# One POOL queue for the first batches' loads, in order of need, and their transposes and scalings reordered, in a fused attention and feed-forward kernel on one Trainium2 core

## The chip, the cores and the metric

The kernel runs on one core of one Trainium2 chip. A core has TensorE (PE in the profile; PEld is its weight load), VectorE (DVE), ScalarE (ACT), GpSimd (POOL) and SyncE (SP), and 16 DMA engines that serve the queues of all of them. The metric is the time on the device in microseconds. For a program on one core it is the time of that core.

## The reference

The inputs are q, k and v of 8 batches with 8 heads, 576 positions and 64 elements a head, gates s of 8 x 8 x 576, and the two weights of a feed-forward layer (512 x 2048 and 2048 x 512). All are float32.

```python
scores = q @ k.T / 8
cum = cumsum(max(s, 0))                      # along the positions
bias = -(cum[i] - cum[j])
scores = where(j > i, -1e9, scores + minimum(bias, 0))
attn = exp(scores - rowmax); attn = attn / (sum(attn) + 1e-9)
x = attn @ v                                 # heads side by side: 4608 tokens x 512
out = gelu_exact(x @ w_in) @ w_out           # 4608 x 512
```

Since the scores are causal, the bias factors into a weight of the key, exp(cum[j]), which cancels the query's share when the row is normalised. The kernel therefore multiplies v and a row of ones by that weight (`wb`), and never forms the bias.

## The kernel before

**Tiling.** The eight heads of a batch form four pairs (`NP`), and one item of work covers a pair: transposes, scores, mask, products with v. The 576 positions are five tiles (`ST`), four of 128 and one of 64. The feed-forward layer runs over 9 chunks (`NCH`) of 512 tokens. Chunk c needs the attention of batch c, and a part of the batch before. The program's order is written out by hand, and every engine and every queue works through its own share of it in that order.

**Loads.** q and k come through POOL's queue, which casts them to bf16 (`load_early`, L105). One call loads one pair, or two pairs with `both`. v comes through SP's queue in float32, one transfer a tile (`load_v`, L183), into two buffers (tag `rawv`). The weights also come through POOL's queue, cast to bf16 (`load_w`, L228). Each kind of queue has eight completion semaphores, so a transfer waits for the one eight before it in its queue to land. Three small copies into `pace` on POOL, and one into `raw_v` (L539), only wait for something and so hold back what follows them in POOL's queue or, through `raw_v`, in SP's.

**Batches 0 and 1.** `tr_item` transposes q or k of one pair on PE: 18 transposes into PSUM (L340), and a copy by DVE into `qkT` (L345). From batch 2 on, DVE rearranges q and k into rows (`interleave`, L156), SP writes those to DRAM (`write_rows`, L165) and reads them back through transposing DMAs (`transpose_rows`, L172).

**Attention of a pair.** `sc_item` makes the scores in two units, each with an Exp on ACT (L363), and masks their diagonal blocks with DVE or POOL (`mask_item`, L372 and L377). `scale_v` multiplies v by its weight on DVE (L211). `av_item` makes numerator and denominator for positions 0 to 511 (L385), and `norm` divides through Ln and Exp on ACT (L402, L403) and a product on DVE into `xT` (L418). `av_rest` and `norm_rest` do the same for positions 512 to 575 of all pairs.

**Feed-forward.** `l1_item` makes two column tiles of the first product (L463) and their Gelu on ACT (L469, L472). `l2_item` makes the second product for 128 tokens (L482), wholly or for some of its 16 steps; after the last step DVE copies it out of PSUM (L489) and SP writes it (L491). In chunks 1 to 6 these products use PSUM tag `mlp`, which has one buffer. Scores and first products share tag `sc` (2 buffers), and transposes, attention products and some others share tag `av` (3 buffers).

**Order of a chunk.** The first layer stands first. Beside it DVE scales v of the next batch, takes maxima of v, q and k (`absmax_v`, L201; `absmax`, L194), and interleaves the batch after next. Then comes the second layer, with the attention of batch c + 1 between its products.

Of the kernel before, what the change touches and what calls it, by code (L numbers as in the profile page):

```python
# [19 lines left out]
def kernel(  # L20
# [10 lines left out]
    nc = tc.nc  # L31
    fp32 = mybir.dt.float32
# [9 lines left out]
    ST = 5  # L42
# [53 lines left out]
    def load_early(b, n, p, both=False):  # L96
        src = q if n == "q" else k
        if p == 0:
            early[b, n] = work.tile([128, 2, 2, G * D], bf16, tag=f"raw{n}", bufs=3, name=f"early_{n}")
        e0 = (p // 2) * 64  # L100
        out = early[b, n][e0 : e0 + 64, p % 2]
        if both:
            out = early[b, n][e0 : e0 + 64].rearrange("g j e f -> g (j e) f")
        ap = [[G * D, 64], [S * D, 4 if both else 2], [1, G * D]]
        nc.gpsimd.dma_start(  # L105
            out=out,
            in_=bass.AP(tensor=src.tensor, offset=src.offset + (b * H + 2 * p) * S * D, ap=ap),
        )
# [5 lines left out]
    for p in range(1, NP):  # L114
        for n in "qk":
            load_early(0, n, p)
    uptri = const.tile([128, 128], fp32, name="uptri")
    make_upper_triangular(nc, uptri, 1.0, diag=True)
    ident_bf = const.tile([128, 128], bf16, name="ident_bf")
    nc.vector.tensor_copy(ident_bf, ident)  # L120
    one = const.tile([64, S], bf16, name="one")
    nc.vector.memset(one, 1.0)
# [12 lines left out]
    for t in vv:  # L135
        nc.vector.memset(t[64:128, ST - 1, :, :], 0.0)
    for t in qkT:
        nc.vector.memset(t[:, 1, :, S:640], 0.0)
# [6 lines left out]
    def load_qk(b):  # L145
        for p in (0, 2):
            for n in "qk":
                load_early(b, n, p, both=True)
# [25 lines left out]
    def v_tile(b):  # L174
        raws[b, "v"] = work.tile([128, ST, H, D], fp32, tag="rawv", bufs=2, name="raw_v")

    def load_v(b, engs):
        if (b, "v") not in raws:
            v_tile(b)
        t = raws[b, "v"]  # L180
        for st in range(ST):
            n_st = 128 if st < ST - 1 else SL
            engs[st % len(engs)].dma_start(  # L183
                out=t[:n_st, st, :, :],
                in_=bass.AP(
                    tensor=v.tensor,
                    offset=v.offset + b * H * S * D + st * 128 * D,
                    ap=[[D, n_st], [S * D, H], [1, D]],
                ),
            )  # L190
# [306 lines left out]
    load_v(0, [nc.sync])  # L497
    exp_set()
    pace = const.tile([128, 1], fp32, name="pace")

    def tr_pair(b, p):
        tr_item(b, p, 0)
        tr_item(b, p, 1)
# [4 lines left out]
    weights_scan()  # L508
    tr_pair(0, 0)
    weights_dve()  # L510
    nc.vector.tensor_copy(tri_bf, uptri)
    sc_item(0, 0, masks=False)
    mask_item(0, 0, 0, nc.vector)
    mask_item(0, 0, 1, nc.gpsimd)
    nc.gpsimd.tensor_copy(pace, raws[0, "v"][:, ST - 3, 0, 0:1])
    for i in range(4):
        load_w(0, i)
    tr_pair(0, 1)
    weights_pe()
    sc_item(0, 1, masks=False)  # L520
    mask_item(0, 1, 1, nc.gpsimd)
    tr_pair(0, 2)
    mask_item(0, 1, 0, nc.vector)
    sc_item(0, 2, masks=False)
    mask_item(0, 2, 1, nc.gpsimd)
    tr_pair(0, 3)
    sc_item(0, 3, masks=False)
    scale_pair(0, 0)
    mask_item(0, 2, 0, nc.vector)
    scale_pair(0, 1)  # L530
    mask_item(0, 3, 0, nc.vector)
    mask_item(0, 3, 1, nc.vector)
    scale_pair(0, 2)
    scale_pair(0, 3)
    for i in range(4):
        load_w(1, i)
    load_qk(1)
    v_tile(1)
    nc.gpsimd.tensor_copy(  # L539
        raws[1, "v"][:, :, 0, 0], w_in_r[:, KO - 1, dff - 1 : dff].to_broadcast([128, ST])  # L540
    )
    load_v(1, [nc.sync])
    for p in range(NP):
        av_item(0, p, wide=p in (1, 2), rest=False)
    nc.gpsimd.memset(amv, 0.0)
    nc.gpsimd.memset(ones, 1.0)
    nc.gpsimd.tensor_copy(pace[:64], raws[1, "v"][:64, ST - 1, 0, 0:1])
    load_qk(2)
    load_qk(3)

    for c in range(NCH):
# [3 lines left out]
        if c == 0:  # L555
            for p in range(NP):
                av_rest(0, p)
            norm_rest(0)
# [3 lines left out]
        if 0 < c and nb < B:  # L562
            if nb + 1 < B:
                load_v(nb + 1, [nc.sync])
            scale_v(nb, STS, nc.vector)
            absmax_v(nb)
# [5 lines left out]
        if 0 < c and nb + 1 < B:  # L572
            for i, n in enumerate("qk"):
                interleave(nb + 1, n)
                write_rows(nb + 1, i, nc.sync)
            if nb + 2 < B:
                nc.gpsimd.tensor_copy(
                    pace, qkT[nb % 2][:, 1, NP - 1, 0:1] if c == 1 else gT_of[c][:, 0, 0:1]
                )
                load_qk(nb + 2)  # L580
        for f2 in range(3, FT // 2):
            l1_item(c, f2)
        if c == 0:
            exp_set()
            l2_item(c, 0, av=True)
            tr_pair(1, 0)
            tr_pair(1, 1)
            l2_item(c, 1, 0, 4)
            tr_pair(1, 2)
            l2_item(c, 1, 4, 8)  # L590
            tr_pair(1, 3)
            sc_item(1, 0)
            l2_item(c, 1, 8)
            load_v(2, [nc.sync])
            sc_item(1, 1)
            l2_item(c, 2, 0, 6, av=True)
            sc_item(1, 2)
            scale_pair(1, 0)
            l2_item(c, 2, 6, 12, av=True)
            sc_item(1, 3)  # L600
            l2_item(c, 2, 12, av=True)
# [24 lines left out]
        elif nb < B:  # L626
            exp_set()
            l2_item(c, 0, 0, 4)
            sc_item(nb, 0)
            l2_item(c, 0, 4)  # L630
            for p in range(1, NP):
# [5 lines left out]
                if p == NP - 1:  # L637
                    if nb + 1 < B:
                        transpose_rows(nb + 1, p)
                    av_item(nb, p)  # L640
# [160 lines left out]
```

## Time and profile before

| | |
|---|---|
| median of 17 runs | 341.06 us (340.38 to 343.04) |
| time of the profiled execution | 341.79 us |
| its span, first to last instruction | 339.9 us |
| PE busy | 318.5 us (94%) |
| DVE / ACT / POOL busy | 197.3 / 202.1 / 35.8 us |
| moved by DMA | 47.30 MB, mean 139 GB/s |

A span is shorter than the time of its execution, since it leaves out what lies before the first and after the last instruction. In a list of instructions in order of time, a line has the start and the duration in microseconds, the engine, the line of the code, the operation, the tiles (out, then in), their shapes and a count. In brackets stands how long the engine was idle before it, and what ended that.

### The profile page before, as it was taken

What the parts mean: (1) busy time and instruction counts of PE and PEld (TensorE: products, weight loads), DVE (VectorE), ACT (ScalarE), POOL (GpSimd) and SP (SyncE); (2) the same over time, 40 slices, a digit from 0 to 9 for tenths busy, and PEclk for the clock granted to TensorE, in tenths of its full rate; (3) what the DMA queues carried; (4) which work ended last, traced back from release to release, by engine and by line L of the source; (5) the groups of instructions that cost most, each with busy time, mean ns of one, the idle gap of its engine ahead of it and who ended that gap; (6) DMA issues with size and microseconds to landing.
All of it is one profiled execution on the core that took longest, in us unless ns stands there. A gap on an engine that the chain in (4) does not pass through costs nothing.

```text
span 339.9 us, 6313 instructions
## 1 busy us (share of the span) xinstructions
PE 318.5 (94%) x2538; PEld 163.2 (48%) x2538; DVE 197.3 (58%) x387; ACT 202.1 (59%) x286; POOL 35.8 (11%) x67
## 2 busy tenths in 40 slices
PE   1778999999899999999999999999999999999993
PEld 1554455644554445445544555455545554444441
DVE  4595756999654964793469446944594456140020
ACT  2566727687567677568657855785768576304400
POOL 7492005000302000020003000000000000000000
PEclk9999999999999999999999999999999999999998
DMA  8999998995798999799769646734500100020011
GB/s 147 152 197 198 197 214 123 210 266 130 154 220 218 108 252 265 156 181 278 184 127 215 207 103 133 139 145 127 102 31 2 62 34 32 16 78 32 3 62 68
DMA packets 88244, 47.30 MB, mean 139 GB/s; under 512 B 68176, under 2 KB 80464, under 8 KB 88208
## 3 DMA queue, kind: packets, MB, share of 16 engines
q1 hardware_dynamic: 75216, 33.19, 41.3%
q0 software_dynamic: 12992, 13.63, 26.3%
q8 instruction: 22, 0.36, 0.4%
q14 instruction: 14, 0.11, 0.1%
HBM read 36.85 MB, written 16.52 MB: 157 GB/s over the span
## 4 chain that ended last, share of the span: by engine, by line
PE 79%; DVE 8%; DMA 5%; ACT 5%; issue 1%; SPq 0%; POOL 0%; ACTq 0%; DVEq 0%; POOLq 0%
PE o_ps L482 35%; PE h_ps L463 27%; PE sc_ps L357 5%; PE avn L385 4%; DMA qkT<-rows 4%; PE avd L385 3%; DMA early_k<-in_k_dram 2%; DVE qkT L345 2%; ACT L469 2%; DVE amx L194 1%; DVE vv L211 1%; PE avw L385 1%; DVE amv L201 1%; ACT gT L469 1%; PE avr L385 1%
## 5 line engine op out<-in xcount | busy, mean ns | idle before, releaser
L482 PE MATMUL o_ps<-w_out_r,gT 128*128 128x512 bf16 x576 | 133.0, 380 | 0.0
L463 PE MATMUL h_ps<-xT,w_in_r 128*128 128x512 bf16 x576 | 126.8, 379 | 2.1 <-ACT gT L469 1.4
L463 PEld LDWEIGHTS <-w_in_r 128*128 128x128 bf16 x576 | 56.0, 98 | 70.5 <-issue 3.5
L363 ACT ACTIVATE P<-sc_ps 128x1024 bf16<-128x1024 f32 x64 | 62.0, 1021 | 42.6 <-PE sc_ps L357 42.5
L482 PEld LDWEIGHTS <-gT 128*128 128x128 bf16 x576 | 53.0, 98 | 60.7
L469 ACT ACTIVATE gT<-h_ps 128x1024 bf16<-128x1024 f32 x54 | 54.3, 1022 | 42.2 <-PE h_ps L463 41.9
L489 DVE COPY o_sb<-o_ps 128x512 f32<-128x512 f32 x36 | 24.7, 687 | 60.0 <-PE o_ps L482 57.3
L372 DVE TENSOR_TENSOR P<-P,tri_bf 128x512 bf16<-128x512 bf16 x61 | 25.6, 423 | 39.2 <-ACT P L363 38.7
L194 DVE TENSOR_REDUCE amx<-qkT 128x2 f32<-128x1152 bf16 x32 | 40.9, 1335 | 0.0
L418 DVE SCALAR_TENSOR_TENSOR xT<-avn,ln 128x256 bf16<-128x256 f32 (+3 forms) x64 | 21.6, 384 | 26.1 <-ACT ln L403 26.1
L211 DVE TENSOR_TENSOR vv<-raw_v,wb 128x512 bf16<-128x512 f32 (+2 forms) x46 | 27.2, 650 | 0.0
L402 ACT ACTIVATE ln<-avd 128x256 f32<-128x256 f32 x56 | 18.6, 391 | 13.5 <-PE avd L385 13.5
L357 PE MATMUL sc_ps<-qkT 64*128 64x256 bf16 (+2 forms) x320 | 22.5, 265 | 4.1 <-DVE qkT L345 3.6
L403 ACT ACTIVATE ln<-ln 128x512 f32<-128x512 f32 (+1 forms) x40 | 23.5, 587 | 1.3
L472 ACT ACTIVATE gT<-h_ps 128x512 bf16<-128x512 f32 x36 | 19.6, 603 | 6.3 <-PE h_ps L463 6.3
L357 PEld LDWEIGHTS <-qkT 64*128 64x128 bf16 x320 | 13.9, 98 | 18.9 <-issue 11.9
L201 DVE TENSOR_REDUCE amv<-raw_v 128x1 f32<-128x2048 f32 (+1 forms) x16 | 22.9, 1470 | 0.0
L385 PEld LDWEIGHTS <-vv 128*64 128x64 bf16 x384 | 17.7, 114 | 9.7 <-issue 4.9
L385 PE MATMUL avn<-P,vv 128*64 128x256 bf16 x224 | 16.8, 273 | 2.3 <-DVE vv L211 1.2
L385 PEld LDWEIGHTS <-wb 128*64 128x64 bf16 x384 | 17.8, 115 | 0.3
L385 PE MATMUL avd<-P,wb 128*64 128x256 bf16 x224 | 15.8, 264 | 0.0
L469 ACT ACT_TABLE_LOAD x8 | 10.3, 1283 | 6.4 <-PE h_ps L463 6.3
(83 smaller groups left out, 137.9 us busy)
## 6 DMA issues: line engine op xcount, KB each, us to landing
out_dram<-o_sb SPq DMA_DIRECT2D x36, 256.0 KB, 2.5
raw_v<-in_v_dram SPq DMA_DIRECT2D x32, 256.0 KB, 6.2
rows<-qk_bf SPq DMA_DIRECT2D x12, 576.0 KB, 4.5
early_q<-in_q_dram POOLq DMA_DIRECT2D x14, 288.0 KB, 8.2
early_k<-in_k_dram POOLq DMA_DIRECT2D x14, 288.0 KB, 9.1
w_in_r<-in_moe_w_in_dram POOLq DMA_DIRECT2D x4, 512.0 KB, 8.2
w_out_r<-in_moe_w_out_dram POOLq DMA_DIRECT2D x4, 512.0 KB, 13.4
raw_v<-in_v_dram SPq DMA_DIRECT2D x8, 128.0 KB, 5.7
```

What stands on the lines that cost most here:

```text
L194: nc.vector.tensor_reduce(amx[:, b * NP + p], qkT[b % 2][:, :, p, :S], axis=AX, op=ALU.max, apply_absolute_value=True)
L201: nc.vector.tensor_reduce(amv[:n_st, b, j : j + 1], t[:n_st, st0:st1].rearrange("p s h d -> p (s h d)"), axis=AX, op=ALU.max, apply_absolu ...
L211: eng.tensor_tensor(vb[:n_st, st0:st1, h0:h1, :], t[:n_st, st0:st1, h0:h1, :], wb[:n_st, st0:st1, b * H + h0 : b * H + h1] .unsqueeze(3).t ...
L357: nc.tensor.matmul(s_ps[:, e, off : off + n], lhsT=qkT[b % 2][e * 64 : e * 64 + 64, 1, p, jt * 128 : jt * 128 + 128], rhs=qkT[b % 2][e * 6 ...
L363: nc.scalar.activation(P[:, :, UO[u] : UO[u] + UW[u]], s_ps[:, :, : UW[u]], func=AF.Exp, scale=scale)
L372: eng.tensor_tensor(d, d, tri_bf.unsqueeze(1).unsqueeze(1).to_broadcast([128, 2, 2, 128]), op=MULT)
L385: nc.tensor.matmul(out[e * 64 : e * 64 + 64, lo : lo + n], lhsT=(wb[:, jt, b * H + h : b * H + h + 1].to_broadcast([128, 64]) if den else ...
L403: nc.scalar.activation(ln[:, :w], ln[:, :w], func=AF.Exp, scale=-1.0)
L463: nc.tensor.matmul(h_of[c, f2][i], lhsT=w_in_r[:, ko, ft * 128 : (ft + 1) * 128], rhs=xT[:, ko, c * NB % XW : c * NB % XW + NB], start=(ko ...
L469: nc.scalar.activation(gT_of[c][:, f2 * 2 : f2 * 2 + 2, :], hh_of[c, f2], func=AF.Gelu)
L482: nc.tensor.matmul(o_ps, lhsT=gT[:, ft, sub * 128 : (sub + 1) * 128], rhs=w_out_r[:, ft, :], start=(ft == 0), stop=(ft == FT - 1),)
L489: nc.vector.tensor_copy(o_sb, o_ps)
```

## The change

It does the following, in the order of the program.

- Every load of q and k covers two pairs. v of every batch goes through POOL's queue, with three buffers instead of two. In that queue stand q and k of batch 0, v of batch 0, w_in, then (behind two masks and three memsets) w_out, q and k of batch 1, v of batch 1, q and k of batch 2. v of batch 2, q and k of batch 3 and v of batch 3 follow in chunk 0. Of the waiting copies on POOL, those of the opening are gone; later ones stand in front of v and of q and k.
- In the opening, transposes of pairs 0 and 1 come before the first scores, and those of pairs 2 and 3 stand one item ahead of their scores. v of batch 0 is scaled by position tiles (one, two, one, one) for all heads, not by pairs. One mask moves from POOL to DVE, and some memsets move or change engine.
- The rest products of batch 0 move from the first layer of chunk 0 to behind its first second-layer product. In that second layer, transposes, scores and second-layer steps of batch 1 are regrouped.
- In chunks 1 to 5 `interleave` and `write_rows` of the batch after next move from the first layer to behind the first score item of the second layer.

```diff
-    def load_early(b, n, p, both=False):
+    def load_early(b, n, p):
 ...
-    for p in range(1, NP):
-        for n in "qk":
-            load_early(0, n, p)
+    for n in "qk":
+        load_early(0, n, 2)
 ...
-    def load_v(b, engs):
-        if (b, "v") not in raws:
-            v_tile(b)
-        t = raws[b, "v"]
+    def load_v(b):
+        t = raws[b, "v"] = work.tile([128, ST, H, D], fp32, tag="rawv", bufs=3, name="raw_v")
         for st in range(ST):
             n_st = 128 if st < ST - 1 else SL
-            engs[st % len(engs)].dma_start(
+            nc.gpsimd.dma_start(
 ...
-    load_v(0, [nc.sync])
 ...
-    weights_scan()
-    tr_pair(0, 0)
-    weights_dve()
-    nc.vector.tensor_copy(tri_bf, uptri)
-    sc_item(0, 0, masks=False)
-    mask_item(0, 0, 0, nc.vector)
-    mask_item(0, 0, 1, nc.gpsimd)
-    nc.gpsimd.tensor_copy(pace, raws[0, "v"][:, ST - 3, 0, 0:1])
+    load_v(0)
+    make_upper_triangular(nc, uptri, 1.0, diag=True)
     for i in range(4):
         load_w(0, i)
-    tr_pair(0, 1)
+    weights_scan()
+    tr_item(0, 0, 0)
+    tr_item(0, 1, 0)
+    weights_dve()
+    tr_item(0, 0, 1)
+    tr_item(0, 1, 1)
     weights_pe()
+    nc.vector.tensor_copy(tri_bf, uptri)
+    for t in vv:
+        nc.vector.memset(t[64:128, ST - 1, :, :], 0.0)
+    sc_item(0, 0, masks=False)
+    tr_item(0, 2, 0)
     sc_item(0, 1, masks=False)
+    tr_item(0, 2, 1)
+    scale_v(0, STS[0:1], nc.vector)
+    tr_item(0, 3, 0)
+    mask_item(0, 0, 0, nc.vector)
+    mask_item(0, 0, 1, nc.vector)
+    sc_item(0, 2, masks=False)
+    tr_item(0, 3, 1)
+    scale_v(0, STS[1:3], nc.vector)
+    mask_item(0, 1, 0, nc.vector)
     mask_item(0, 1, 1, nc.gpsimd)
+    scale_v(0, STS[3:4], nc.vector)
+    sc_item(0, 3, masks=False)
+    mask_item(0, 2, 0, nc.vector)
 ...
     for i in range(4):
         load_w(1, i)
     load_qk(1)
-    v_tile(1)
-    nc.gpsimd.tensor_copy(
-        raws[1, "v"][:, :, 0, 0], w_in_r[:, KO - 1, dff - 1 : dff].to_broadcast([128, ST])
-    )
-    load_v(1, [nc.sync])
+    load_v(1)
+    load_qk(2)
 ...
-        if c == 0:
-            for p in range(NP):
-                av_rest(0, p)
-            norm_rest(0)
 ...
-            if nb + 1 < B:
-                load_v(nb + 1, [nc.sync])
 ...
-        if 0 < c and nb + 1 < B:
-            for i, n in enumerate("qk"):
-                interleave(nb + 1, n)
-                write_rows(nb + 1, i, nc.sync)
+        if 1 < c and nb + 1 < B:
+            nc.gpsimd.tensor_copy(pace, gT_of[c][:, 0, 0:1])
+            load_v(nb + 1)
             if nb + 2 < B:
-                nc.gpsimd.tensor_copy(
-                    pace, qkT[nb % 2][:, 1, NP - 1, 0:1] if c == 1 else gT_of[c][:, 0, 0:1]
-                )
                 load_qk(nb + 2)
 ...
         if c == 0:
             exp_set()
+            load_v(2)
+            load_qk(3)
+            load_v(3)
             l2_item(c, 0, av=True)
-            tr_pair(1, 0)
-            tr_pair(1, 1)
-            l2_item(c, 1, 0, 4)
-            tr_pair(1, 2)
-            l2_item(c, 1, 4, 8)
-            tr_pair(1, 3)
+            for p in range(NP):
+                av_rest(0, p)
+            norm_rest(0)
+            l2_item(c, 1, 0, 8)
 ...
             l2_item(c, 0, 0, 4)
             sc_item(nb, 0)
+            if nb + 1 < B:
+                for i, n in enumerate("qk"):
+                    interleave(nb + 1, n)
+                    write_rows(nb + 1, i, nc.sync)
             l2_item(c, 0, 4)
 ...
+                    if c == 1:
+                        nc.gpsimd.tensor_copy(pace, qkT[(nb + 1) % 2][:, 1, p, 0:1])
+                        load_qk(nb + 2)
```

## The prediction

> **What bounds the kernel now.** I read the page first, then busy time by stretches, then the instructions in order of time in the opening and after one block's first matmul.
>
> ```profile
> span 339.9 us, 6313 instructions
> PE 318.5 (94%) x2538; PEld 163.2 (48%) x2538; DVE 197.3 (58%) x387; ACT 202.1 (59%) x286; POOL 35.8 (11%) x67
> ...
> PE   1778999999899999999999999999999999999993
> ```
>
> ```profile
> 0.00:26.80 26.80, 15.16 (x253) 11.76 (x254) 17.44 (x36) 13.63 (x21) 19.16 (x34) 1.00 1.01 168
> 26.80:34.28 7.48, 6.25 (x60) 2.85 (x57) 3.86 (x6) 4.77 (x9) 0.99 (x4) 1.00 1.21 195
> ...
> 173.60:208.60 35.00, 34.71 (x266) 17.66 (x264) 22.42 (x43) 23.93 (x35) 2.65 (x5) 1.00 0.74 166
> ```
>
> The columns after the length are the busy us of PE, PEld, DVE, ACT and POOL. A later block of 35.0 us has 0.29 us of idle PE; the opening 26.8 us has 11.6. So time can be won only before about 34 us, and any new PE wait in a later block is paid in full.
>
> The opening, in order of time (start, duration):
>
> ```profile
> 5.37 0.69 PE L340 MATMUL tr_ps<-ident_bf,early_q 64*64 64x64 bf16 x18 [5.37 <-DMA early_q<-in_q_dram]
> ...
> 18.80 2.75 DVE L211 TENSOR_TENSOR vv<-raw_v,wb 128x512 bf16<-128x512 f32 x2
> ...
> 19.38 1.18 POOL L372 TENSOR_TENSOR P<-P,tri_bf 128x512 bf16<-128x512 bf16 x1
> ...
> 21.18 0.96 PE L385 MATMUL avn<-P,vv 128*64 128x256 bf16 x8 [1.21 <-DVE vv L211]
> ...
> 22.93 0.66 ACT L402 ACTIVATE ln<-avd 128x256 f32<-128x256 f32 x2 [1.40 <-PE avd L385]
> ...
> 28.48 0.75 DVE L418 SCALAR_TENSOR_TENSOR xT<-avn,ln 128x256 bf16<-128x256 f32 x2 [0.45 <-ACT ln L403]
> ...
> 34.28 8.79 PE L463 MATMUL h_ps<-xT,w_in_r 128*128 128x512 bf16 x40 [0.56 <-ACT gT L469]
> ```
>
> The path runs from the landed q and k through transposes, PSUM copies and scores to DVE's scaling of v, the attention products, the Ln and Exp of ACT (from 22.93) and the last xT (29.23). A later block, where a second-layer product hands over its PSUM tile:
>
> ```profile
> 157.65 0.22 DVE L377 TENSOR_TENSOR P<-P,tri_bf 128x128 bf16<-128x128 bf16 x1
> 157.65 0.57 PE L385 MATMUL avn<-P,vv 128*64 128x256 bf16 x8
> 157.78 0.68 DVE L489 COPY o_sb<-o_ps 128x512 f32<-128x512 f32 x1
> ...
> 158.66 3.63 PE L482 MATMUL o_ps<-w_out_r,gT 128*128 128x512 bf16 x16
> ```
>
> Tag mlp has one buffer, so the matmuls at 158.66 can't start before the copy of the product before them ends (158.46). The slack is 0.2 us.
>
> **What the Trainium skill says.** "SBUF — State Buffer", section "Who interferes with whom": a DVE instruction with two SBUF inputs and a GpSimd one that reads SBUF exclude each other. The trace agrees: the first scaling above took up to 2.33 us beside POOL's mask, against a mean of 0.73. "DMA: Bandwidth & Descriptors", section "Issuing engines are not separate DMA queues": a transfer moved from SP's queue to POOL's runs on the same 16 engines. The trace agrees: both queues together held them at or above full share, so the move changes order, not bandwidth. "TensorE: Matmul & The Clock Gate", Part 1: the array runs at half rate until some microseconds of steady work. Here 18 transposes took 0.69 us in the opening and 0.47 at 46 us, although the clock column says 1.00; earlier attention products stay slow.
>
> **The change, part by part.**
>
> Landing of q, k, v. Between 0 and 14 us the DMA engines moved 2.40 MB at 172 GB/s, nearly all of it q, k and v of batch 0. In order, the first q (now 288 KB) lands about 4.1 us after issue, the least that early_q shows: 5.3, as now. At 204 GB/s (the rate at 18 to 30 us) each further 288 KB takes 1.45 us: k at 6.8, the other pairs at 8.3 and 9.8. v in 256-byte packets on POOL's queue is not in the trace. SP's packets cost 19 ns at 68 to 72 us and 23 in the opening; POOL's 1 KB packets 97 ns. So v's 4608 packets on 16 engines take 5.5 to 28 us. I take 6, since a 1 KB packet reads 2 KB of fp32: tile 3 at about 15, all at 16, as now (pace waited for v until 14.6). Their issue: 0.63 us for 256 runs, 0.78 for 512, hence about 1.07 for 1024; five take 5.1, from 4.3 to 9.4. uptri comes behind them, at 10.2, and DVE's tri_bf waits for it.
>
> DVE decides the opening. Scan from 4.2 (1.28), four copies at 0.72 and cum (0.50) to 9.5; tri_bf to 10.4; two vv memsets (0.27) to 11.0; the copy of q pair 2 to 11.7. That of k pair 2 waits for PE, whose scores of pair 1 wait for ACT's second exponential (11.5): 13.4. Then tile 0 (0.67), q pair 3 (0.72), masks of pair 0 (1.06) and k pair 3 (0.72): 16.6; tiles 1 and 2 (1.35), a mask (0.42) and tile 3 (0.67): 19.1. POOL's two masks (1.6 each) collide with these: 0.5 to 1.6, I take 1.0: 20.1. ACT's exponentials are no longer last: eight of 0.97 end near 19 (now 21.5). The first products finish 1.0 later, at 21.1 instead of 22.9: **1.8 us earlier**. The chain to the last xT keeps its length. Removed from 30.3 are the 0.62 us of rest products and the 0.56 us wait for the first Gelu, whose table load no longer follows the rest's Exp: 1.8 + 0.6 + 0.6 = 3.0 at 34.28. Off the path: the other memsets and mask moves.
>
> Second layer of chunk 0. The rest products return: 0.6. Between the four score items stand 16 matmuls instead of 20, 0.86 us less cover for eight exponentials (7.8 us); about 0.5 shows as PE wait. Left: **1.9 us** gained (bounds 0 and 5: no lead at all, or products bound by ACT alone, den at 18.2). Weights, q, k and v of batch 1 stay hidden: in order at 204 GB/s w_out lands by 36 (used from 40), q and k by 42 (used from 45), v by 48 (used from 55).
>
> Later blocks. Interleave of the next batch moves from before the first masks to between them and the o_sb copy, in the blocks of chunks 1 to 5. It issues four DVE copies of 0.44, 1.47 end to end, and two row writes on SP. Behind it in DVE's queue stands the o_sb copy, and PE waits for that: copy from 159.25 to 159.93, PE on at 160.0 instead of 158.66: **1.35 us**. Nothing takes it back, since PE was busy throughout. Chunk 1 shows this in another place today:
>
> ```profile
> 85.66 0.81 DVE L156 COPY qk_bf<-early_q 128x1152 bf16<-128x1152 bf16 x2
> ...
> 86.39 0.81 DVE L156 COPY qk_bf<-early_k 128x1152 bf16<-128x1152 bf16 x2
> 87.13 0.74 DVE L372 TENSOR_TENSOR P<-P,tri_bf 128x512 bf16<-128x512 bf16 x2
> 87.60 0.69 PE L385 MATMUL avn<-P,vv 128*64 128x256 bf16 x8 [1.09 <-DVE P L372]
> ```
>
> There the wait is swapped: 1.35 against today's 1.09, with 0.2 us of natural delay before it, net 0.06. In chunk 2 a wait of 0.31 for a DMA transpose goes: net 1.04. Sum: 0.06 + 1.04 + 3 x 1.35 = **5.15 us**. SP's row writes come 2.5 us later, but the transposes have some 20 us until the next block's scores; what else SP had, the v loads, is gone from its queue, and POOL's paces and loads end before the interleave.
>
> Sum: -1.9 + 5.15 = +3.25. The profiled span of 339.9 becomes 343.15. That execution's own time, 341.79, lies 1.9 above its span and 0.7 above the median of the runs; applied to the median 341.06, the sum gives **344.3**.
>
> **Rivals.**
> 1. v on POOL's queue is slow (30 ns a packet, as when both queues share): each batch of v takes 3 us more, the opening lead falls to 0.5, and v of batch 3 still loads when batch 2's transposes run; those took over 10 us beside loads at 109 to 122. With 2 us of waiting for them: 341.06 - 0.5 + 5.15 + 2 = 347.7. Against it: 19 ns alone.
> 2. The other side: the interleave stays hidden. If the first masks end 1.15 us sooner, or the slack after the copy is 1.35 instead of 0.2, PE doesn't wait, and today's 1.09 and 0.31 go too: 341.06 - 1.9 - 1.4 = 337.8. Against it: the masks follow ACT's table load and Exp, which follow PE's own first layer.
> 3. The opening gains its bound, 5: 341.06 - 5 + 5.15 = 341.2, no change. It needs POOL's masks and uptri never to hold DVE.
>
> **How the numbers follow.** My forecast has 0.66 (342.0 to 346.3: lead of 4.2 down to 0, stalls a little more or less); rival 1 0.16 (346 to 351); rival 2 0.10; rival 3 0.08 (340.4 to 341.7). From 340.5 to 347.5 lie the forecast, rival 3 and a third of rival 1: 8 in 10. 0.2% is 0.7 us, about what a measurement can tell: faster 0.10, same 0.08, slower 0.82.
>
> **What would show it.** Right: in five blocks o_ps matmuls waiting about 1.35 us for o_sb, with qk_bf between L377's and o_sb's rows; the first Ln near 21; no h_ps wait for Gelu near 33; first v landed by 12. Wrong: no wait on o_sb, a first Ln before 19 or after 22.5, or PE waiting for raw_v, w_out or qkT.

## The result, and the profile after

The changed kernel takes 346.84 us (median of 8 runs, 345.76 to 347.41), the kernel before 340.99 us beside it (47 runs). The ratio is 1.016, 95% interval 1.0140 to 1.0181: slower by 5.8 us. The forecast was 344.3 us, with a range up to 347.5. The sign and the main mechanism were right. The size was 2.5 us short, and the range held in part by luck: 346.84 lies above the 342.0 to 346.3 that the prediction gave to its own mechanism, in the part that it gave to rival 1, whose slow loads did not come. Two more executions are on record, the profiled one with 346.45 and one with 349.6 us, at a mean granted clock of 0.996 and 0.989.

The page of the changed kernel, with the costliest group of instructions at the end (busy us, mean ns of one, then the idle time of the engine just before them and what ended it). Before, that last column was 0.0:

```profile
span 344.7 us, 6308 instructions
...
PE 318.7 (92%) x2538; PEld 163.4 (47%) x2538; DVE 196.9 (57%) x385; ACT 201.7 (59%) x286; POOL 66.7 (19%) x100
...
L472 PE MATMUL o_ps<-w_out_r,gT 128*128 128x512 bf16 x576 | 133.1, 380 | 6.3 <-DVE o_sb L479 6.3
```

PE has the same busy time as before, 318.7 against 318.5 us, in a span 4.8 us longer. The second-layer products, which never waited before, now idle 6.3 us for DVE's copy of the product ahead. PE's waits (us in total, times, longest) give the place of each:

```profile
PE o_ps L472 <- DVE o_sb L479: 6.3, 5, 1.3
...
PE sc_ps L347 <- DVE qkT L335: 3.3, 2, 3.0
PE h_ps L453 <- ACT gT L459: 1.2, 4, 0.3
```

Five waits of up to 1.3 us, one in each of the blocks of chunks 1 to 5; the wait for qkT lies in the opening, and those for gT follow further down. This is one of them, in order of time (the line numbers of the changed kernel are ten lower than those of before):

```profile
157.36 0.22 DVE L367 TENSOR_TENSOR P<-P,tri_bf 128x128 bf16<-128x128 bf16 x1
...
157.50 0.82 DVE L151 COPY qk_bf<-early_q 128x1152 bf16<-128x1152 bf16 x2
...
158.24 0.82 DVE L151 COPY qk_bf<-early_k 128x1152 bf16<-128x1152 bf16 x2
...
158.97 0.68 DVE L479 COPY o_sb<-o_ps 128x512 f32<-128x512 f32 x1
...
159.71 3.61 PE L472 MATMUL o_ps<-w_out_r,gT 128*128 128x512 bf16 x16 [1.26 <-DVE o_sb L479]
```

Between the mask (start 157.36) and the o_sb copy (158.97) DVE now runs the four copies of the interleave. The copy ends at 159.65, and the next second-layer product starts at 159.71 after 1.26 us of idle. Before, the o_sb copy started 0.13 us after the mask did.

The opening of the changed kernel, the lines that answer to those shown before, with both of POOL's large masks and a small mask of DVE:

```profile
13.72 1.15 POOL L362 TENSOR_TENSOR P<-P,tri_bf 128x512 bf16<-128x512 bf16 x1 [0.98 <-ACT P L353]
13.80 1.62 DVE L201 TENSOR_TENSOR vv<-raw_v,wb 128x512 bf16<-128x512 f32 x1
...
16.61 1.15 POOL L362 TENSOR_TENSOR P<-P,tri_bf 128x512 bf16<-128x512 bf16 x1 [0.91 <-ACT P L353]
16.68 1.17 DVE L367 TENSOR_TENSOR P<-P,tri_bf 128x128 bf16<-128x128 bf16 x1
...
21.81 0.66 ACT L392 ACTIVATE ln<-avd 128x256 f32<-128x256 f32 x2 [0.65 <-PE avd L375]
...
27.33 0.76 DVE L408 SCALAR_TENSOR_TENSOR xT<-avn,ln 128x256 bf16<-128x256 f32 x2 [0.45 <-ACT ln L393]
```

The first Ln starts at 21.81 (22.93 before) and the last xT ends at 28.09 (29.23 before). No first-layer product waits for the Gelu near 33 us.

Put side by side by stage (a stage starts with its first `h_ps` or `o_ps` product in the list in order of time):

| us | before | after | difference | predicted |
|---|---|---|---|---|
| up to the first h_ps | 26.80 | 25.56 | -1.24 | -1.8 |
| chunk 0, first layer | 16.11 | 14.75 | -1.36 | -1.2 |
| chunk 0, second layer | 24.78 | 26.13 | +1.35 | +1.1 |
| chunk 1, second layer | 22.02 | 22.06 | +0.04 | +0.06 |
| chunk 2, second layer | 21.11 | 22.06 | +0.95 | +1.04 |
| chunks 3, 4, 5, second layer, each | 20.74 | 22.06 | +1.32 | +1.35 |
| chunk 6, first layer | 13.81 | 14.27 | +0.46 | 0 |
| from the last second layer's start to the end | 19.78 | 20.42 | +0.64 | 0 |
| all other stages together | | | 0 | 0 |

The differences add up to +4.8, the difference of the spans. The medians differ by 5.8, since the profiled execution of before was one of the slower ones (341.79 against a median of 341.06), and that of after one of the faster (346.45 against 346.84). So the comparison of these two profiles makes the opening look some 1 us better than it is, which the runs below confirm.

### The profile page after: what moved, and what is told of

It reads as the page before. It is cut to its first block, busy times and chain, and to the rows that moved or that the text cites. A ratio compares the mean times of both kernels' runs of the same rounds, so it can differ in the third digit from the quotient of the medians.

```text
span 344.7 us, 6308 instructions
## 1 busy us (share of the span) xinstructions
PE 318.7 (92%) x2538; PEld 163.4 (47%) x2538; DVE 196.9 (57%) x385; ACT 201.7 (59%) x286; POOL 66.7 (19%) x100
## 2 busy tenths in 40 slices
DMA packets 53621, 47.30 MB, mean 137 GB/s; under 512 B 31249, under 2 KB 43537, under 8 KB 53585
## 3 DMA queue, kind: packets, MB, share of 16 engines
q1 hardware_dynamic: 37712, 23.75, 26.5%
## 4 chain that ended last, share of the span: by engine, by line
PE 74%; DVE 11%; ACT 10%; DMA 2%; issue 1%; DVEq 0%; POOL 0%; ACTq 0%; POOLq 0%
PE o_ps L472 32%; PE h_ps L453 30%; ACT P L353 4%; PE avn L375 3%; PE sc_ps L347 3%; PE avd L375 3%; DVE qk_bf L151 2%; DVE vv L201 2%; DVE amv L191 2%; DMA early_k<-in_k_dram 2%; ACT L459 1%; ACT L484 1%; DVE amx L184 1%; PE avw L375 1%; ACT gT L462 1%
## 5 line engine op out<-in xcount | busy, mean ns | idle before, releaser
L362 DVE TENSOR_TENSOR P<-P,tri_bf 128x512 bf16<-128x512 bf16 x62 | 25.6, 421 | 43.7 <-ACT P L353 43.5
L173 POOL DMA_DIRECT2D raw_v<-in_v_dram x40 | 34.8, 890 | 12.4 <-DMA w_out_r<-in_moe_w_out_dram 6.8
L347 PE MATMUL sc_ps<-qkT 64*128 64x256 bf16 (+2 forms) x320 | 22.9, 265 | 4.3 <-DVE qkT L335 3.3
L201 DVE TENSOR_TENSOR vv<-raw_v,wb 128x512 bf16<-128x512 f32 (+2 forms) x43 | 26.2, 664 | 0.0
L191 DVE TENSOR_REDUCE amv<-raw_v 128x1 f32<-128x2048 f32 (+1 forms) x16 | 22.9, 1470 | 0.0
L554 POOL CAST pace<-gT 128x1 f32<-128x1 bf16 x4 | 0.8, 198 | 84.8 <-ACT gT L459 84.8
```

The costliest lines, as they stand in the source:

```text
L173: nc.gpsimd.dma_start(out=t[:n_st, st, :, :], in_=bass.AP(tensor=v.tensor, offset=v.offset + b * H * S * D + st * 128 * D, ap=[[D, n_st], ...
L191: nc.vector.tensor_reduce(amv[:n_st, b, j : j + 1], t[:n_st, st0:st1].rearrange("p s h d -> p (s h d)"), axis=AX, op=ALU.max, apply_absolu ...
L201: eng.tensor_tensor(vb[:n_st, st0:st1, h0:h1, :], t[:n_st, st0:st1, h0:h1, :], wb[:n_st, st0:st1, b * H + h0 : b * H + h1] .unsqueeze(3).t ...
L347: nc.tensor.matmul(s_ps[:, e, off : off + n], lhsT=qkT[b % 2][e * 64 : e * 64 + 64, 1, p, jt * 128 : jt * 128 + 128], rhs=qkT[b % 2][e * 6 ...
L362: eng.tensor_tensor(d, d, tri_bf.unsqueeze(1).unsqueeze(1).to_broadcast([128, 2, 2, 128]), op=MULT)
```

## The experiments

All times are medians beside runs of the kernel before on the same chip, whose medians were 341.03 to 341.33. Each is of 4 to 22 executions, except for run h, which was a single one.

**Run a: the interleave behind the copy.**

```diff
             sc_item(nb, 0)
-            if nb + 1 < B:
-                for i, n in enumerate("qk"):
-                    interleave(nb + 1, n)
-                    write_rows(nb + 1, i, nc.sync)
             l2_item(c, 0, 4)
+            if nb + 1 < B:
+                for i, n in enumerate("qk"):
+                    interleave(nb + 1, n)
+                    write_rows(nb + 1, i, nc.sync)
```

> The changed kernel, with the interleave and its row writes of the blocks of chunks 1 to 5 put behind the o_sb copy of the first second-layer product instead of ahead of it; nothing else. Theory (the copy stands behind four DVE copies, and PE stands behind the copy): the five waits for o_sb of 1.3 us go, and the blocks of chunks 1 to 5 fall from 22.06 us to 20.74 each; 5 x 1.32 = 6.6 us less than the changed kernel, 346.8 - 6.6 = 340.2, a little below the kernel before. Rival (the time is lost to the order of the POOL queue, v behind q and k, and the wait for o_sb only shows it): the same 346.8, with the wait under another name. Second rival (the interleave delays whatever stands behind it, here the masks of the next pair): some of the 6.6 comes back as a wait for P or qkT, 342 to 345.

339.93 us, ratio 0.995 (0.9931 to 0.9970): 6.9 us less than the changed kernel, where the five second layers were 6.6 us longer. All five took 20.74 us here, and no wait for o_sb or P, nor a new one for qkT, took the place of the old ones. In chunk 3, the copy of the product now stands ahead of the interleave:

```profile
156.79 0.68 DVE L479 COPY o_sb<-o_ps 128x512 f32<-128x512 f32 x1
157.39 0.82 DVE L151 COPY qk_bf<-early_q 128x1152 bf16<-128x1152 bf16 x2
157.67 3.63 PE L472 MATMUL o_ps<-w_out_r,gT 128*128 128x512 bf16 x15
```

The interleave costs DVE the same 1.5 us here; only what stands behind it in DVE's queue is different. Both rivals fall. It already beats the kernel before: the 1.09 us that the interleave cost chunk 1 in its old place are gone too, and so is the wait of 0.31 us in chunk 2.

**Run b: the interleave's move alone, in the kernel before.**

```diff
         if 0 < c and nb + 1 < B:
-            for i, n in enumerate("qk"):
-                interleave(nb + 1, n)
-                write_rows(nb + 1, i, nc.sync)
 ...
             sc_item(nb, 0)
+            if nb + 1 < B:
+                for i, n in enumerate("qk"):
+                    interleave(nb + 1, n)
+                    write_rows(nb + 1, i, nc.sync)
             l2_item(c, 0, 4)
```

> The kernel before, with only the interleave and its row writes of the later blocks moved to where the changed kernel has them; opening, v on SP and the paces stay as before. Theory: the five waits for o_sb appear here too, net of the two waits of before (1.09 and 0.31) 0.04 + 0.95 + 3 x 1.32 = 4.95 us, so 341.0 + 4.95 = 345.9. Rival (the POOL queue's order, or the later paces, cost the time): no more than 0.5 us over the kernel before, 341.0 to 341.5.

345.92 us, ratio 1.0140 (1.0115 to 1.0165): +4.6 us by the medians, +4.8 by the ratio. One edit brings about five sixths of the loss. Its waits of PE:

```profile
PE o_ps L482 <- DVE o_sb L489: 6.3, 5, 1.3
```

The same 6.3 us, five times, as in the changed kernel, with v on SP and the old opening.

**Run c: the pace on another tile.** What made chunk 6's first layer 0.46 us longer? The list of ACT's waits of the changed kernel has an entry without a tile, which is the table load in front of a chunk's first Gelu (us in total, times, longest):

```profile
ACT L459 <- PE h_ps L453: 8.5, 4, 2.1
```

Chunk 6 of the changed kernel, in order of time:

```profile
247.89 0.42 ACT L393 ACTIVATE ln<-ln 128x256 f32<-128x256 f32 x1
...
250.42 1.28 ACT L459 ACT_TABLE_LOAD   x1 [2.12 <-PE h_ps L453]
...
252.79 3.40 PE L453 MATMUL h_ps<-xT,w_in_r 128*128 128x512 bf16 x15 [0.29 <-ACT gT L459]
```

ACT is idle from 248.3, and yet loads the Gelu's table only when the first products are done, at 250.42. The Gelu writes gT, and the pace copy of the chunk before reads gT on POOL, so it waits for two engines. In the trace the wait for PE is then an instruction of its own, ahead of the table load, and the Gelu itself waits only for POOL. In the kernel before this happened in chunks 3, 4 and 5, in the changed one in chunk 6 as well, since there is a pace in one more chunk.

```diff
-            nc.gpsimd.tensor_copy(pace, gT_of[c][:, 0, 0:1])
+            nc.gpsimd.tensor_copy(pace, vv[nb % 2][:, 0, 0, 0:1])
```

> The changed kernel, with POOL's pace copy of chunks 2 to 5 reading the scaled v of the next batch instead of the first Gelu's output; nothing else. Theory (the pace makes the next chunk's first Gelu wait on two engines, and its table load then starts only after the product): the first Gelu of chunks 3 to 6 has its table loaded ahead, and their first layers fall from 14.27 to 13.81; 4 x 0.46 = 1.8 us less, 346.8 - 1.8 = 345.0. Rival (the late table load has to do with the Exp ahead of it, or is hidden): 346.8, the four waits unchanged.

344.94 us: 1.9 less than the changed kernel, 1.8 expected. The entry above is gone from ACT's waits, and the first layers of chunks 3 to 6 take 13.81 us. Chunk 6 in this run:

```profile
247.66 0.42 ACT L393 ACTIVATE ln<-ln 128x256 f32<-128x256 f32 x1
248.09 1.28 ACT L459 ACT_TABLE_LOAD   x1
```

The table load follows the Exp at once, and PE has no wait for gT left.

**Run d: the changed kernel with the interleave in its old place.**

```diff
+        if 0 < c and nb + 1 < B:
+            for i, n in enumerate("qk"):
+                interleave(nb + 1, n)
+                write_rows(nb + 1, i, nc.sync)
         if 1 < c and nb + 1 < B:
             nc.gpsimd.tensor_copy(pace, gT_of[c][:, 0, 0:1])
 ...
             sc_item(nb, 0)
-            if nb + 1 < B:
-                for i, n in enumerate("qk"):
-                    interleave(nb + 1, n)
-                    write_rows(nb + 1, i, nc.sync)
             l2_item(c, 0, 4)
```

> The changed kernel, with the interleave back in the first layer of chunks 1 to 5, where the kernel before has it; so what is left of the change is its opening, v on the POOL queue and the paces. Theory: opening and second layer of chunk 0 give -1.26, the fourth late table load +0.46, in the blocks the waits of before come back; 341.0 - 1.26 + 0.46 = 340.2, up to 340.8 if the 0.6 us by which the closing of the program was longer in the profile belongs to the change. Prediction's own step: -1.9, so 339.1. Rival (the opening gains nothing, its lead is given back): 341.0 or more.

341.65 us (22 runs, 340.44 to 345.78), ratio 1.0019 (1.0003 to 1.0036). Take off the 0.46 us of the fourth late table load, and opening and v loads are worth nothing. The expectation of 340.2, read from one pair of profiles, failed, and so did the prediction's 339.1. The four longest of the 22 runs, 343.5 to 345.8 us, are also the four with the lowest mean granted clock, 0.986 to 0.992. The wait of 0.31 us in chunk 2 is gone here as well, with the interleave in its old place, so that place alone doesn't make it.

**Runs e and f: both edits, with the new and with the old opening.**

Run e is the changed kernel with the edits of a and of c. Run f is the kernel before with this:

```diff
         if 0 < c and nb + 1 < B:
-            for i, n in enumerate("qk"):
-                interleave(nb + 1, n)
-                write_rows(nb + 1, i, nc.sync)
 ...
-                    pace, qkT[nb % 2][:, 1, NP - 1, 0:1] if c == 1 else gT_of[c][:, 0, 0:1]
+                    pace, qkT[nb % 2][:, 1, NP - 1, 0:1] if c == 1 else vv[nb % 2][:, 0, 0, 0:1]
 ...
             l2_item(c, 0, 4)
+            if nb + 1 < B:
+                for i, n in enumerate("qk"):
+                    interleave(nb + 1, n)
+                    write_rows(nb + 1, i, nc.sync)
```

> The changed kernel with both edits: the interleave behind the o_sb copy, and the pace of chunks 2 to 5 on the scaled v. Theory: the two savings don't touch each other, so 339.9 - 1.85 = 338.1, with the first layers of chunks 3 to 6 at 13.81 us and the second layers of chunks 1 to 5 at 20.74. Rival (a new limit shows as soon as both are gone, such as the transposes through SP): 339 to 340.

> The kernel before (its opening, its queues) with the same two edits. It measures what the changed opening and the v loads on POOL's queue are worth with all else equal. Theory of the runs so far (the opening's lead of about 1.2 us at the first h_ps is spent on a pause of PE of 1.2 to 1.3 us between the transposes of batch 1, in three executions of four): equal to the run with the changed opening within 0.5 us, so 338.0 to 338.6. The prediction's own step (the opening gains 1.9): 1.9 us slower than that run, 340.0.

e: 338.50 us, ratio 0.9922 (0.9903 to 0.9941). f: 338.27 us, ratio 0.9914 (0.9894 to 0.9934). The two edits nearly add up (338.1 expected), and with both in place the new opening is no faster than the old. Before chunk 1's first layer starts, the executions with the old opening (before, b, f) took 67.69, 66.58 and 67.18 us, mean 67.2; those with the new one (after, a, c, d, e) 66.43, 68.35, 67.55, 66.81 and 66.86, mean 67.2. On average the new opening leads by 0.6 us at the first h_ps and gains 1.6 more in chunk 0's first layer, and all of it is lost again in chunk 0's second layer, in two ways. One was predicted (rest products and fewer products between the scores). The other was not: in a, c and d, PE stood still in the middle of a group of 18 transposes. In e, which had no pause, 0.3 us of lead over f were left when chunk 1 started, and the stage that closes the program, 20.3 us against 20.0, took them.

**Where PE's pause comes from.** PE's waits in that stretch in run a:

```profile
PE tr_ps L330 <- issue: 1.3, 1, 1.3
```

```profile
48.62 0.35 PE L330 MATMUL tr_ps<-ident_bf,early_k 64*64 64x64 bf16 x11
50.32 0.28 PE L330 MATMUL tr_ps<-ident_bf,early_k 64*64 64x64 bf16 x7 [1.34 <-issue]
```

"issue" means that the profile shows nothing that PE waits for. 11 of the 18 transposes ran, the other 7 came after 1.34 us of idle. What the DMA view does show is a packet of another kind just before (packets, MB, share of 16 engines):

```profile
q8 instruction: 1, 0.02, 5.8%
```

Queue q8 brings 0.36 MB in 22 packets in every kernel of this study, 16 KB each. The Trainium skill, "Runtime: NRT & Kernel Launch", section "Instruction fetch mechanics", says that an engine fetches its instructions in blocks of 16 KB, 256 instructions, through its own DMA queue, and that this is mostly hidden. The size agrees, and so does the spacing of packets in the kernel before, on average 240 profiled PE instructions over the first eight. Here it isn't hidden. In this table, "begun" counts the matmuls and weight loads of PE before the packet's start, as the busy times by stretches list them:

| run | packet starts, us | begun | it takes, us | pause of PE, us | second layer of chunk 0 |
|---|---|---|---|---|---|
| before | 44.74 | 717 | 0.92 | none | 24.78 |
| f | 44.19 | 717 | 0.92 | none | 24.79 |
| e | 47.45 | 816 | 1.32 | none | 25.96 |
| after | 47.05 | 840 | 1.10 | 0.2 | 26.13 |
| h (below) | 45.92 | 855 | 1.46 | 1.0 | 28.54 |
| d | 47.13 | 887 | 1.38 | 1.2 | 27.30 |
| c | 47.97 | 887 | 1.42 | 1.2 | 27.30 |
| a | 47.53 | 889 | 1.38 | 1.3 | 28.73 |

The pause always comes at the same instruction, and ends a nearly fixed time after the packet: in c, a, d and h PE goes on 1.40, 1.41, 1.54 and 1.59 us after the packet's end, though those ends lie between 47.4 and 49.4 us. The changed kernel has a short pause there too. Its 18 transposes at that place took 0.64 us, the group before them 0.47:

```profile
49.31 0.64 PE L330 MATMUL tr_ps<-ident_bf,early_k 64*64 64x64 bf16 x18
```

It went on 1.51 us after the packet's end. In e, PE got there 1.3 us after the packet's end and was held for less than 0.1 us; in before, f and g, it got there 2.6 us or more after it, and nothing held it. The place fits as well: 958 matmuls and weight loads stand ahead of it, 241 more than the 717 at which the packet starts in before, which is one packet by the spacing of 240. So the pause is a wait for this packet.

Why the packet is late is less sure. In the changed order PE goes quickly through 64 short instructions of the rest products and then through five groups of transposes and into a sixth, so it gets to the next packet's instructions sooner. Meanwhile the packet may stand among v's and q's packets, in DMA engines that are busy throughout. In a and h the granted clock falls after the pause, which costs about as much again; in c and d it stays at 1.00. Run a in stretches of 2 us (the column before the last two is the clock):

```profile
50.00:52.00 2.00, 1.68 (x35) 0.98 (x36) 1.15 (x2) 0.00 (x0) 1.36 (x2) 0.93 1.19 238
52.00:54.00 2.00, 2.00 (x33) 1.27 (x29) 1.63 (x3) 0.87 (x1) 0.63 (x1) 0.50 1.22 281
54.00:56.00 2.00, 1.78 (x12) 0.72 (x11) 0.98 (x3) 1.07 (x2) 0.62 (x1) 0.72 1.00 213
```

**Run g: v of batch 1 on SP again** (run e otherwise).

```diff
     def load_v(b, eng=nc.gpsimd):
         t = raws[b, "v"] = work.tile([128, ST, H, D], fp32, tag="rawv", bufs=3, name="raw_v")
+        if b == 1:
+            nc.gpsimd.tensor_copy(
+                t[:, :, 0, 0], w_in_r[:, KO - 1, dff - 1 : dff].to_broadcast([128, ST])
+            )
 ...
-    load_v(1)
+    load_v(1, nc.sync)
```

> As the run with both edits, but v of batch 1 goes through SP's queue as in the kernel before (ahead of it a POOL copy into the tile, so that it starts after w_in); all other loads stay on POOL. Theory (PE's own instruction packet of 16 KB, wanted when PE has begun about 720 of its instructions, is late behind v in POOL's queue): the packet starts near 720 to 730 instructions, as in the kernel before, instead of 844 to 893; the pause of 1.2 us is gone and the second layer of chunk 0 takes 26.1 us or less; 1 us faster than the run with both edits. Rival (the pause comes from something else in that stretch, such as the transposes' PSUM copies): the pause stays.

353.15 us, ratio 1.0350 (1.0323 to 1.0378), 14.7 us slower than e instead of 1 faster. The pause was gone: the packet started at 46.11 us with 745 instructions begun and took 0.92 us. But PE waited for v instead:

```profile
PE avn L379 <- DVE vv L205: 6.9, 1, 6.9
```

It waited another 4.0 us for v before the next pair's products, and from 64 to 76 us the granted clock was 0.50. The five tiles of v landed between 39.2 and 70.8 us, where on POOL's queue in e they had come between 44.6 and 50.8. From 39 to 65 us POOL's packets took 90.5% of the engines' time and SP's 26.5%. The miss is about the price of the edit. For the pause the run is in favour of the packet, but it changed the load on the DMA engines too much to settle it.

**Run h: no masks on POOL in the opening** (run e otherwise). It leaves out two masks that the result needs, only to price the meeting of POOL and DVE.

```diff
-    mask_item(0, 1, 1, nc.gpsimd)
-    mask_item(0, 2, 1, nc.gpsimd)
```

> As the run with both edits, but the two masks of batch 0 that POOL multiplies in the opening (second unit of pairs 1 and 2) are left out altogether, so the rows above the diagonal of those pairs are not zeroed there. It prices the meeting of POOL and DVE. Theory of the prediction (collisions cost 1.0, bounds 0.5 to 1.6): the scaling of tile 0 and the masks of pair 1 fall to their lone durations and the first Ln comes 1.0 to 1.5 us sooner than 21.8. Rival (the path runs over PE and ACT there, DVE has room): less than 0.3 us.

338.68 us; what counts is the opening, in order of time:

```profile
14.24 0.68 DVE L201 TENSOR_TENSOR vv<-raw_v,wb 128x512 bf16<-128x512 f32 x1
...
16.18 0.22 DVE L367 TENSOR_TENSOR P<-P,tri_bf 128x128 bf16<-128x128 bf16 x1
...
20.36 0.66 ACT L392 ACTIVATE ln<-avd 128x256 f32<-128x256 f32 x2 [0.66 <-PE avd L375]
```

From the start of the first scaling to the first Ln it is 6.12 us, against 8.01 in the changed kernel and in e. The 1.89 us are two meetings: the scaling takes 0.68 instead of 1.62 us, the small mask 0.22 instead of 1.17. Each is held for most of a POOL mask of 1.15 us. This execution paid for its lead with a pause of 1.0 us and a slow clock behind it, in the second layer of chunk 0.

**Runs i and j: the rest products early, then all masks on DVE.**

Run i is run e with the first of these edits, run j is run i with the second.

```diff
         l1_item(c, 1, 0, KO - 1)
+        if c == 0:
+            for p in range(NP):
+                av_rest(0, p)
 ...
-            for p in range(NP):
-                av_rest(0, p)
             norm_rest(0)
```

```diff
+    scale_v(0, STS[3:4], nc.vector)
-    mask_item(0, 1, 1, nc.gpsimd)
-    scale_v(0, STS[3:4], nc.vector)
+    mask_item(0, 1, 1, nc.vector)
 ...
-    mask_item(0, 2, 1, nc.gpsimd)
-    scale_v(0, STS[4:5], nc.vector)
+    mask_item(0, 2, 1, nc.vector)
 ...
         av_item(0, p, wide=p in (1, 2), rest=False)
+        if p == 1:
+            scale_v(0, STS[4:5], nc.vector)
```

> As the run with both edits, but the 32 rest products of batch 0 stand in the first layer of chunk 0 again, where the kernel before has them; their Ln, Exp and xT stay where the change put them. In the changed order 64 quick PE instructions (32 products and their weight loads) stand between the request of PE's instruction packet and the transposes that need it. Theory (the pause is that packet, late behind POOL's loads): with them moved ahead, PE has some 7 us more work before it needs the packet, so no pause between the transposes; the 0.6 us of the rest products lies in PE's wait for the last xT; the second layer of chunk 0 takes 25.3 us or less; 338.5 - 0.6 - about 0.7 for the pauses of some executions = 337.2. Rival (the pause has another cause): it stays in this execution or the next, and the time falls by 0.6 at most, 337.9 to 338.5.

> As the run before it, and in the opening the two masks of POOL (second unit of pairs 1 and 2 of batch 0) are multiplied by DVE, just after the scaling of v tile 3 and after pair 2's first mask; the scaling of tile 4, which only the rest products read, moves behind the second xT. Theory (POOL and DVE hold each other up: without POOL's masks the first Ln came 1.9 us sooner after the first scaling): DVE's 2 x 0.6 us for the masks lie behind the products of pair 0, so the first Ln comes 1.5 to 1.9 us sooner than in the changed opening and the whole ends 1.5 us sooner, 335.7. Rival (DVE is then full and the last xT is late by what the masks take): 337.0.

i: 337.31 us, ratio 0.9888 (0.9865 to 0.9911), 1.2 us less than e, 1.3 expected. The packet started with 720 instructions begun, there was no pause, the second layer took 25.20 us, and all six runs lay within 0.6 us. v stayed on POOL's queue: a different order of PE's own short instructions is enough to have the packet in time.

j: 336.43 us, ratio 0.9867 (0.9834 to 0.9901), 0.9 less than i instead of 1.5. The first Ln came at 20.37 and chunk 1 started 1.1 us sooner than in i, but a new wait took most of that back in the profiled execution:

```profile
PE sc_ps L347 <- DMA qkT<-rows: 1.1, 1, 1.1
```

```profile
68.28 11.09 SPq L167 DMA_TRANSPOSE qkT<-rows  x4
```

The first four transposes of batch 2 held SP's queue for 11.1 us while q, k and v of batch 3 came in on POOL's, v until 78.2 us.

**Runs l and m: v of batch 3 later** (run j otherwise).

Both take it out of chunk 0, where it stands behind `load_qk(3)`. Run l puts it at the end of chunk 1, run m into chunk 1's first layer.

```diff
             load_qk(3)
-            load_v(3)
 ...
                         nc.gpsimd.tensor_copy(pace, qkT[(nb + 1) % 2][:, 1, p, 0:1])
+                        load_v(3)
                         load_qk(nb + 2)
```

```diff
+        if c == 1:
+            nc.gpsimd.tensor_copy(pace, qkT[nb % 2][:, 1, NP - 1, 0:1])
+            load_v(nb + 1)
 ...
             load_qk(3)
-            load_v(3)
```

> As the run with the rest products early and all masks of the opening on DVE, but v of batch 3 is loaded behind chunk 1's pace, with q and k of batch 4, instead of in chunk 0. There the transposes of batch 2, issued on SP at 68.3 us, took 11.1 us for four beside POOL's loads, and PE waited 1.1 us for qkT before the scores of batch 2. Theory (prediction's first rival: late transposes of batch 2 collide with v of batch 3): the wait for qkT goes, 336.4 - 1.0 = 335.4, and the executions lie closer together than 335.6 to 338.9. Rival (the transposes are late because SP issues them late, whatever loads): the wait stays in most executions, 336.4.

> As the run before it, but v of batch 3 is loaded in chunk 1 already, paced on the last qkT transpose of batch 2 (which landed at 83 us) instead of on batch 3's. Theory: v is there by about 91 us, before DVE scales it at 103, so neither the wait for qkT of 1.1 us nor the wait for P of 3.8 us is left, and chunks 1 and 2 take 20.74 us in their second layers; 336.4 - 1.0 = 335.4. Rival (v's 5 us of load meets the row writes and transposes of batch 3 at 84 to 100 us and makes those late): a wait for qkT in chunk 2 instead, 336 to 338.

l: 341.71 us, ratio 1.0006 (0.9985 to 1.0027), a miss by 6. The wait for qkT was gone, as the theory had it, and the second layer of chunk 1 took 20.74 us again. But v landed only at 106.8 to 112.2 us, and DVE, whose queue has the scaling of v ahead of the next masks, was late with those:

```profile
PE avn L375 <- DVE P L362: 3.8, 1, 3.8
```

The second layer of chunk 2 took 25.89 us, 5.15 more than the others: the wait, and then a granted clock of 0.65 and 0.50 in the two stretches of 2 us from 120 us on. m puts the load between the two, behind batch 2's last transpose. 335.39 us, as expected, ratio 0.9838 (0.9814 to 0.9862), five runs within 1.4 us:

```profile
span 333.6 us, 6260 instructions
```

Neither wait is left. m beats the changed kernel by 11.4 us and the kernel before by 5.8.

## Why the prediction was right or wrong

**The interleave between masks and copy: right, with its size.** Predicted 1.35 us a block, 0.06 net in chunk 1, 1.04 in chunk 2, 5.15 in all; measured 1.32, 0.04 and 0.95, 4.95 in all, and 4.6 to 4.8 by run b alone. The step that carried it was to name what stands behind the moved copies in DVE's queue (the o_sb copy) and who waits for that (PE, for the single buffer of tag mlp). Run a shows that it was this place and not the work. Rival 2, that it stays hidden, fell with five waits in the profile; rival 3 fell with the opening's lead.

**The opening's lead: wrong in size.** Predicted 1.9 us net; e against f gives -0.2 us, nothing. Four terms of the sum failed.

First, the 22.93 of before that the lead was measured from was one late execution: b and f, with the same opening, had 21.86 and 22.45. This, too, is POOL meeting DVE. In all three the first Ln comes 1.4 us after the end of the first scaling of v, and that scaling took 2.75 us in before and 2.50 in f, with two of POOL's large masks beside it, and 1.76 in b, with one. Against the mean of the three, 22.4, the changed opening (21.1 to 22.9 in five executions) leads by 0.5 us.

Second, "collide with these: 0.5 to 1.6, I take 1.0": the meetings of POOL and DVE cost 1.89 us (run h), above the upper end, because each of two DVE instructions was held for some 0.95 us of POOL's mask of 1.15. The cited section "Who interferes with whom" has the rule; its price was set too low, though the 2.33 us against 0.73 that the prediction quotes already show one scaling held for 1.6 us. Other terms of DVE's sum were too long, which hid most of this error: from the landing of q to the first Ln the prediction reckons with 15.8 us, and the five executions took 15.9 to 16.3. They differ mainly by that landing, at 5.1 to 6.9 us.

Third, the pause in the second layer of chunk 0, which isn't in what the prediction let that stage give back, takes another 1.3 to 2.8 us in some executions (27.30 to 28.73 against 25.96). Fourth, the stage that closes the program, put at nothing, is some 0.4 us longer with the new loads.

**The later paces: a step missed.** "POOL's paces and loads end before the interleave" was true and beside the point. What a pace reads was not asked: one more chunk whose pace reads gT holds one more table load, 0.46 us, as run c shows.

**Rival 1: half right.** v on POOL's queue was not slow at the start: its five tiles of batch 0 landed from 11.7 to 16.3 us, about as forecast, but not in packets of 256 bytes, since the whole kernel has 53,621 packets now and had 88,244 before. Its second half, v of batch 3 meeting batch 2's transposes, didn't show in the changed kernel but came up in run j, where PE reached those scores sooner.

**The sum.** 344.3, plus 2.1 for the lead that wasn't there (1.9 forecast, -0.2 measured by e against f, the closing stage included), plus 0.46 for the table load, minus 0.2 to 0.5 for stalls a little smaller, is 346.4 to 346.7; measured 346.84.

## What to carry to other kernels

When work moves on an engine that isn't the bottleneck, look at the instruction behind it in that engine's queue and at who waits for its result; the same 1.5 us of DVE copies cost 1.3 us a block ahead of a PSUM copy and nothing behind it. Don't read a gain of 1 us out of one execution on each side: the first h_ps behind one and the same opening came at 25.6 to 26.8 us (before, b and f). A wait that only paces a queue also ties the tile that it reads to that queue, so let it read one that nobody needs to overwrite soon.

## What the runs showed of the hardware

- PE can stand still for 1.0 to 1.3 us with no semaphore to wait for, when it runs through hundreds of short instructions while the DMA engines are full. It then waits for its own instruction packet of 16 KB, and goes on 1.4 to 1.6 us after that packet's end (runs a, c, d, h and the changed kernel). The packet starts up to 170 instructions later than elsewhere (887 to 889 begun against 717). When it was asked for isn't in the trace, so that it stood behind other packets is inferred.
- After such a pause the granted clock fell to 0.50 to 0.72 for some 4 us in run a, and the two together lengthened the stage by 2.8 us against e. It fell to 0.50 after the waits of 3.8 us in run l and 6.9 us in run g as well, and did not fall after the pauses of 1.2 us in c and d.
- A table load in front of an activation that waits for two engines started only after the first wait: 1.28 us that lay behind the products instead of beside them, and a first layer 0.46 us longer (14.27 against 13.81 in run c).
- The tiles of v of one batch landed within 6.2 us of each other on POOL's queue (run e) and within 31.6 us on SP's beside a busy POOL queue (run g). In the latter, from 39 to 65 us, the two queues had about as many packets (3,250 on POOL's, 3,446 on SP's), but 4.47 MB went through POOL's and 1.00 through SP's.
- A DVE instruction with two SBUF inputs beside a POOL mask of 1.15 us was held for 0.95 us, twice (run h against the changed kernel).
- Stays open: from the last second layer's start to the end, executions with v on POOL's queue took 20.3 to 20.6 us, those of the three kernels with the old loads 19.8 to 20.0, though all products and copies there keep their distances. The difference lies behind the last product.
